# A one-core attention and MLP kernel: each engine's sequence and each tile's buffer taken from two tables instead of from a planner

## The chip, the core and the metric

The kernel runs on one core of a Trainium2 chip. A core has five engines that run their own instruction queues side by side and wait for each other through semaphores: TensorE (PE, matrix multiplies; its weight loads are listed apart as PEld), VectorE (DVE), ScalarE (ACT), GpSimd (POOL) and SyncE (SP, which here only issues DMAs). Each engine takes its instructions strictly in the order in which the program lists them; so an instruction that waits holds up all that stand behind it on that engine. SBUF is the working memory, PSUM the eight banks into which PE writes.

The metric is the device time of one execution in microseconds (us). Before the change the median of 3 runs is 272.35 us (272.06 to 272.52).

## The reference, cut to what matters

```python
batch, n_heads, seq, head_dim = (4, 8, 768, 64)

def _attn_ref(q, k, v):
    chunk = 32; nc = S // chunk; top_k = 6
    k_chunks = k.reshape(B, H, nc, chunk, D)
    k_min = np.min(k_chunks, axis=3)
    k_max = np.max(k_chunks, axis=3)
    ub = np.sum(np.maximum(q * k_min, q * k_max), axis=-1)      # per query and chunk
    ub = np.where(causal, ub, -1000000000.0)
    top_chunks = np.argsort(ub, axis=-1)[..., -top_k:]
    scores = scale * np.matmul(q, k.transpose(0, 1, 3, 2))
    mask = sel & (pos[:, None] >= pos[None, :])                 # sel: key's chunk is chosen
    attn = softmax(np.where(mask, scores, -1000000000.0))
    return np.matmul(attn, v)

def _moe_ref(x, w_in, w_out):       # x: 3072 tokens x 512; d_ff = 2048
    h = x @ w_in
    g = np.where(h > 0.0, h, np.exp(np.minimum(h, 0.0)) - 1.0)
    return g @ w_out
```

Attention over the six best chunks of 32 keys for each query, then an MLP with ELU on the result.

## The kernel before, in words

**Units.** The 32 heads (4 batches of 8) are handled as 16 *pairs* u = 0 to 15; four pairs make a batch. Rows are handled in two *halves* of 384 (hf = 0, 1). Below, K0 is the K load of pair 0 in its first half and K0' in its second; Q and V likewise.

**Stages.** For the first batch (pairs 0 to 3) `first_prep` loads K, Q and V of one half each (L701 and L710), turns each K or Q block on PE with an identity matrix (L730, here called a *turn*), and copies the result out of PSUM with ACT (L759 for K as `lhs`, L779 for Q as `qt`, L784 for its positive part `qa`); DVE takes the minima and maxima of the chunks (L765), POOL copies Q into `rhs` (L799 to L801) and V into `vext` (L792). For the other batches `pair_prep` loads the two K and Q blocks in small pieces (L623), and DVE turns them (L636, L654). `quad_sel` works for two pairs at once: PE makes the bounds (L821 to L833), DVE transposes them, finds the sixth largest (L862) and marks the chunks below it (L867, L873), POOL copies these marks into `rhs` (L884, the *selection copies*). `pair_attend` makes scores on PE (L921 to L931), exponentials on ACT (`pt`, L952), the causal edge on POOL (L971) or PE, the product with V on PE (PV, L979 to L984), the division on DVE (L997, L1000), a transpose on PE (L1009) and its copy by ACT (`xT`, L1012). `mlp` then makes, per batch and half, 16 up-projections (L1034; groups of four matmuls), the ELU on ACT and DVE (L1044 to L1078), 12 down-projection parts for three blocks of rows (L1097), a copy by ACT (`osb`, two buffers, L1105) and the store (L1109 on SP). The weights w_in and w_out come in four parts each by DMAs that POOL issues (L592, L596), each held back until a given product of the first batch exists (`gates`).

**Queues.** Nearly all loads and all stores are issued by SP; ACT issues the two Q loads of pairs 0 and 1. The order on SP is the order of the transfers' issue; a load whose buffer isn't free holds up everything behind it on SP.

**Buffers.** Every tile has a class with a fixed number of buffers (`caps`): 3 `stage`, 9 `pt`, 3 `e`, 2 `osb`, 8 `xT` and so on. PSUM's eight banks are four pairs: pair 0 always holds wide tiles (two banks), pair 1 single ones, pairs 2 and 3 change between both uses; `part` makes a new pool at each such change.

**What sets the order.** The program first records 1706 operations with `add`: engine, an estimated duration, a priority, what they read and write, the buffers that they take and free. Then `Plan.order` (L187) plays a list scheduler: it holds clocks for the engines, a picture of the DMA queues and of instruction fetches, and takes at each step the operation that could start first, ties by priority; a table `RANKS` shifts the priorities of some 300 operations beforehand. It returns the operations in order, each with the buffer numbers that it got, and the program emits them in that order.

Of the kernel before, what the change touches and what calls it, by code (L numbers as in the profile page):

```python
# [42 lines left out]
def WHEN(q_in, left, out):  # L43
# [7 lines left out]
WARM = 8  # L51
# [7 lines left out]
RANKS = ((0, 1, 127), (11, 1, 71), (17, 1, -43), (33, 1, -100), (37, 1, -51), (48, 1, 127), (49, 1, -12),  # L59
# [54 lines left out]
DUMP = None  # L114
# [5 lines left out]


class Plan:

    LAT = {"PE": 0.21, "ACT": 0.17, "DVE": 0.13, "POOL": 0.08, "SP": 2.2, "POOLQ": 2.5}

    BEGIN = 0.85  # L130
    COLD = 7.0
    RING = 2560
    LANES = 8
# [1065 lines left out]
```

## Time and profile before

| what | value |
|---|---|
| median of 3 runs | 272.35 us (272.06 to 272.52) |
| the profiled execution, first to last instruction | 276.5 us, 4.15 us above that median |
| mean granted clock of PE over the span | 0.974 of full speed |
| PE, DVE, ACT, POOL busy | 96%, 72%, 73%, 45% of the span |
| DMA | 29.81 MB, mean 108 GB/s |
| longest waits on PE | 1.3 us (DVE memset ahead of the warming matmuls), then 0.8 us and less |

How to read it: a busy share is that of instructions in flight; matmuls overlap, and a PE that is busy is not at its peak. The granted clock is a row of its own. In timelines, the brackets at a line's end give the idle time of the engine ahead of it and what ended that. SP's lines show when a DMA was issued, not when it landed.

### The profile page before, as it was taken

Reading aid. Unit: us, or ns where it says so; the run is one execution under the profiler, and the core shown is the slowest. Engines: PE = TensorE matmul, PEld = TensorE weight load, DVE = VectorE, ACT = ScalarE, POOL = GpSimd, SP = SyncE. Lnnn points to the kernel's source line nnn. Section 1 sums busy time; section 2 is a strip of 40 time slices with the busy share of each in tenths; the row PEclk is TensorE's granted clock in tenths of the full one; section 3 lists DMA queues with packets and bytes.
Section 4 is the critical chain, followed back from the end, with each engine's and each line's share of the span. In section 5 each row is a group of like instructions: output and inputs, shape, how many; then the busy total and the mean of one; then the engine's idle time right before and its main releaser. Section 6 shows DMA issues by size and latency. Waiting matters only on the chain.

```text
span 276.5 us, 6918 instructions
## 1 busy us (share of the span) xinstructions
PE 266.1 (96%) x2573; PEld 165.0 (60%) x2600; DVE 198.8 (72%) x526; ACT 202.8 (73%) x382; POOL 124.5 (45%) x219
## 2 busy tenths in 40 slices
PE   8889998899999999999999999999999999999995
PEld 4778855565555565655556565666556655555544
DVE  5944686995998998799699953876884846615920
ACT  2956799994797899988979989779579744435411
POOL 5783182794687499766537776010062200000000
PEclk9965899999999999999999999999999999999999
DMA  7999989499997999999974301101010111011022
GB/s 183 235 236 189 189 124 167 73 162 152 149 235 112 199 149 183 177 173 153 158 168 79 78 2 38 40 0 40 10 70 0 40 39 38 28 51 38 2 76 76
DMA packets 111473, 29.81 MB, mean 108 GB/s; under 512 B 101072, under 2 KB 108496, under 8 KB 111440
## 3 DMA queue, kind: packets, MB, share of 16 engines
q1 hardware_dynamic: 106800, 24.78, 48.2%
q0 software_dynamic: 4224, 4.19, 9.8%
q8 instruction: 20, 0.33, 0.5%
q10 hardware_dynamic: 416, 0.39, 0.5%
q14 instruction: 13, 0.11, 0.1%
HBM read 27.26 MB, written 6.29 MB: 121 GB/s over the span
## 4 chain that ended last, share of the span: by engine, by line
PE 71%; DMA 10%; DVE 5%; ACT 5%; issue 3%; SPq 2%; POOL 2%; ACTq 0%; DVEq 0%; POOLq 0%
PE psM L1097 17%; PE psH L1034 15%; PE psS L925 10%; PE psS L1034 8%; PE psMT L1097 7%; PE psO L984 6%; DMA gT<-in_q_dram 4%; DMA w_out_sb<-in_moe_w_out_dram 3%; ACT pt L952 2%; PE psS L833 2%; PE psT L1009 2%; PE psH L735 2%; DMA stage<-in_q_dram 2%; DMA stage<-in_k_dram 1%; SPq L712 1%
## 5 line engine op out<-in xcount | busy, mean ns | idle before, releaser
L952 ACT ACTIVATE pt<-psS 128x768 bf16<-128x768 f32 (+1 forms) x120 | 90.0, 788 | 9.1 <-PE psS L925 7.8
L1034 PE MATMUL psH<-xT,w_in_sb 128*128 128x384 bf16 x384 | 72.9, 325 | 0.1
L1097 PE MATMUL psM<-w_out_sb,gT 128*128 128x512 bf16 x264 | 68.2, 379 | 1.6 <-DMA w_out_sb<-in_moe_w_out_dram 0.2
L1034 PEld LDWEIGHTS <-w_in_sb 128*128 128x128 bf16 x512 | 48.2, 97 | 32.8 <-issue 0.9
L971 POOL TENSOR_SCALAR_AFFINE_SELECT pt<-pt 128x256 bf16<-128x256 bf16 (+1 forms) x56 | 28.8, 518 | 65.5 <-ACT pt L952 64.2
L925 PE MATMUL psS<-rhs,lhs 88*128 88x384 bf16 (+4 forms) x304 | 55.3, 292 | 1.6 <-ACT pt L952 0.7
L1097 PEld LDWEIGHTS <-gT 128*128 128x128 bf16 x400 | 37.1, 97 | 33.0 <-issue 1.2
L1044 ACT ACTIVATE e<-psH 128x384 f32<-128x384 f32 x96 | 47.0, 513 | 8.9 <-PE psH L1034 7.2
L925 PEld LDWEIGHTS <-lhs 88*128 88x128 bf16 x304 | 28.8, 101 | 17.0 <-issue 2.5
L984 PEld LDWEIGHTS <-pt 128*128 128x128 bf16 x672 | 28.5, 99 | 9.6 <-issue 1.7
L1073 DVE SCALAR_TENSOR_TENSOR t<-e,psH 128x384 bf16<-128x384 f32 x48 | 25.5, 545 | 12.1 <-ACT e L1044 11.9
L801 POOL CAST rhs<-qt 64x768 bf16<-64x768 f32 (+1 forms) x40 | 27.9, 701 | 13.3 <-ACT qt L779 11.5
L884 POOL COPY rhs<-selt 24x576 bf16<-24x576 bf16 (+2 forms) x40 | 22.6, 564 | 25.0 <-DVE selt L873 23.3
L984 PE MATMUL psO<-vext,pt 128*128 128x65 bf16 x672 | 32.1, 196 | 0.3 <-POOL pt L971 0.2
L1052 DVE SCALAR_TENSOR_TENSOR gT<-e,psH 128x384 bf16<-128x384 f32 x48 | 25.3, 540 | 9.7 <-ACT psH L1049 9.6
L1044 ACT ACTIVATE e<-psS 128x768 f32<-128x768 f32 x16 | 13.0, 810 | 18.4 <-PE psS L1034 18.4
L1078 DVE SCALAR_TENSOR_TENSOR gT<-psH,t 128x384 bf16<-128x384 f32 x48 | 25.5, 545 | 0.5
L1049 ACT ACTIVATE psH<-psH 128x384 f32<-128x384 f32 x48 | 24.5, 522 | 0.0
L801 POOL CAST lhs<-kt 64x768 bf16<-64x768 f32 x24 | 19.9, 831 | 6.7 <-DVE kt L636 4.5
L1034 PE MATMUL psS<-xT,w_in_sb 128*128 128x384 bf16 x128 | 22.4, 326 | 0.0
L1097 PE MATMUL psMT<-w_out_sb,gT 128*128 128x512 bf16 (+1 forms) x109 | 22.1, 348 | 0.2
L1012 ACT ACTIVATE xT<-psT 128x384 bf16<-128x384 bf16 x32 | 15.8, 501 | 8.6 <-PE psT L1009 8.5
(66 smaller groups left out, 287.6 us busy)
## 6 DMA issues: line engine op xcount, KB each, us to landing
out_dram<-osb SPq DMA_DIRECT2D x23, 256.0 KB, 2.0
stage<-in_k_dram SPq DMA_DIRECT2D x48, 96.0 KB, 3.6
stage<-in_q_dram SPq DMA_DIRECT2D x48, 96.0 KB, 3.8
vd<-in_v_dram SPq DMA_DIRECT2D x12, 384.0 KB, 4.7
w_in_sb<-in_moe_w_in_dram POOLq DMA_DIRECT2D x4, 512.0 KB, 8.4
w_out_sb<-in_moe_w_out_dram POOLq DMA_DIRECT2D x4, 512.0 KB, 9.5
gT<-in_v_dram SPq DMA_DIRECT2D x16, 96.0 KB, 5.1
gT<-in_k_dram SPq DMA_DIRECT2D x6, 192.0 KB, 5.0
```

Of the source, the lines that this page charges most:

```text
L801: nc.gpsimd.tensor_copy(out=o, in_=i)
L925: nc.tensor.matmul(p_s[:, hd, pc:pc + w], lhsT=tiles[pt_["kb"]][0:64 + NCH, hd, 128 * kb:128 * kb + 128], rhs=tiles[pt_["qb"]][0:64 + NCH, ...
L952: lambda bs=bs, pt=pt, wtot=wtot, lo=lo, at=at: nc.scalar.activation(out=tiles[pt][:, :, lo:lo + wtot], in_=tiles[bs[0]][:, :, at:at + wto ...
L971: nc.gpsimd.affine_select(out=a, in_=a, compare_op=AOT.is_ge, fill=0.0, base=0, pattern=pat, channel_multiplier=-1)
L984: nc.tensor.matmul(po[:, hd, qi, :], lhsT=tiles[pt][:, hd, off:off + 128], rhs=tiles[pt_["vx"]][:, 6 * hd + kb, :], start=(kb == 0), stop= ...
L1034: nc.tensor.matmul(ph, lhsT=w_in_sb[:, kk, f0:f0 + 128], rhs=tiles[XT[4 * b + kk]][:, c0:c0 + HALF], start=(kk == 0), stop=(kk == NKK - 1))
L1044: lambda e=e, view=view: nc.scalar.activation(out=tiles[e][:, 0:step], in_=view(), func=AF.Exp),
L1049: lambda view=view: nc.scalar.activation(out=view(), in_=view(), func=AF.Relu),
L1052: lambda e=e, view=view, fc=fc, gt=gt: nc.vector.scalar_tensor_tensor(out=tiles[gt][:, fc:fc + step, :], in0=tiles[e][:, 0:step], scalar=1 ...
L1073: lambda e=e, t=t, view=view: nc.vector.scalar_tensor_tensor(out=tiles[t][:, 0:step], in0=tiles[e][:, 0:step], scalar=1.0, in1=view(), op0 ...
L1078: lambda t=t, view=view, fc=fc, gt=gt: nc.vector.scalar_tensor_tensor(out=tiles[gt][:, fc:fc + step, :], in0=view(), scalar=0.0, in1=tiles ...
L1097: nc.tensor.matmul(pm, lhsT=tiles[gt][:, fc, 128 * tt:128 * tt + 128], rhs=w_out_sb[:, fc, cs], start=(fc == 0), stop=(fc == NFC - 1))
```

## The change

The planner is taken out: `RANKS`, the constants of its clock, DMA and fetch pictures, the hook `DUMP`, and the whole body of `order`. In their place stand two tables: `ORDER` lists the 1706 operations by number in the order in which they are emitted, and `SLOTS` lists the buffer of each tile in the order of its taking. The operations themselves, their shapes, their reads and writes, the buffer counts and every other constant are unchanged.

```diff
-RANKS = ((0, 1, 127), (11, 1, 71), (17, 1, -43), (33, 1, -100), (37, 1, -51), (48, 1, 127), (49, 1, -12),
...
-DUMP = None
+ORDER = (
+    0, 4, 13, 33, 3, 15, 31, 6, 67, 185, 49, 1, 2, 51, 69, 19, 10, 169, 11, 17, 7, 43, 20, 8, 21, 221, 9, 25, 44,
...
+)
+
+SLOTS = (
+    0, 1, 2, 0, 2, 3, 0, 0, 0, 4, 1, 0, 1, 0, 5, 1, 0, 0, 1, 0, 3, 2, 1, 1, 2, 0, 2, 6, 3, 1, 1, 1, 7, 1, 2, 2, 0,
...
+)
...
     def order(self):
-        ops = self.ops
-        for first, n, shift in RANKS:
-            for o in ops[first:first + n]:
-                o.prio += 0.02 * shift
...
-        return out
+
+        left = iter(SLOTS)
+        return [(self.ops[i], [(h, next(left)) for h in self.ops[i].alloc]) for i in ORDER]
...
     steps = plan.order()
-    if DUMP is not None:
-        DUMP(steps)
     with tc.manual_schedule():
```

The lines of the changed kernel stand some 163 lower than those of the kernel before (L706 is L543, L1097 is L934).

Set against the order that the planner gives, each engine has the same operations in another sequence:

| engine | operations | mean shift in places | largest shift |
|---|---|---|---|
| PE | 574 | 3.2 | 22 |
| DVE | 368 | 2.3 | 21 |
| ACT | 383 | 2.5 | 44 |
| POOL | 205 | 4.4 | 40 |
| SP | 83 | 2.4 | 19 |

The head of SP's queue (places 1 to 26; each V of this part is two DMAs):

```
before  K0 K1 Q2 V0 K2 K3 Q3 V1 V2 V3 Q0' K1' Q1' K0' Q3' K3' K2' Q2' V3' V1' V0' V2' K4 Q4 Q5 K5
after   K0 K1 K3 K1' K2 Q2 Q3 Q0' V0 K3' Q2' V2 K0' V1 Q1' V3 K2' Q3' V0' V1' V2' Q5 K4 K5 Q4 V3'
```

The head of PE's queue (places 0 to 21; t: turn, s and S: first and second scores of a pair's first half, ub: bounds of two pairs, pv: the product with V):

```
before  tK0 tQ1 tK1 tQ0 tK2 tQ2 tK3 tQ3 s1 ub01 s2 s0 tQ0' s3 ub23 tK1' S0 S1 tK0' pv0 pv0 tQ1'
after   tK0 tQ1 tQ0 tK1 tK2 tQ2 tK3 tQ3 s1 ub01 tK1' tQ0' s0 s2 ub23 tK0' S0 s3 S1 tQ1' pv0 pv1
```

On POOL the eight requests for weights stand at places 13, 14, 30, 31, 42, 43, 56, 57 before and at 14, 26, 27, 32, 45, 48, 58, 61 after. On SP the first store moves from place 32 to 38, behind the loads K8, K9, Q8 and Q9, of which none stood ahead of it. The first up-projection keeps its place 55 on PE.

More of the change, by code (lines that the diff above doesn't have):

```diff
@@ L128 @@
     LAT = {"PE": 0.21, "ACT": 0.17, "DVE": 0.13, "POOL": 0.08, "SP": 2.2, "POOLQ": 2.5}
[L130 to L133, printed above, removed]
-    FETCH = (120, 256, 4.5, 0.95, 434, 1.5)
-    SHARE = {"SP": 1.0, "ACT": 1.0, "POOL": 0.64}
-    WAKE = 1.2
     def __init__(self, caps):
@@ L187, in order @@
     def order(self):
-        ops = self.ops
-        for first, n, shift in RANKS:
-            for o in ops[first:first + n]:
-                o.prio += 0.02 * shift
-        for o in ops:
-            o.left = len(o.deps) + len(o.after)
-            o.ready = 0.0
-            o.start = o.end = None
-            for d in o.deps:
-                d.users.append(o)
-            for d in o.after:
-                d.followers.append(o)
-        free_slots = {c: [(0.0, i) for i in range(n)] for c, n in self.caps.items()}
@@ L201, in order @@
-        banks = [0.0] * self.caps["ps"]
-        held = {}
-        engines = {}
-        def back(h, t):
-            if h[0] == "ps":
-                banks[held[h]] = t
-            elif h[0] == "S2":
-                banks[2 * held[h]] = banks[2 * held[h] + 1] = t
-            else:
-                free_slots[h[0]].append((t, held[h]))
-        def vacant(c):
-            if c == "ps":
-                return min(banks[2:])
-            if c == "S2":
-                return min(max(banks[i], banks[i + 1]) for i in range(0, len(banks), 2) if i != 2)
-            return min(free_slots[c])[0] if free_slots[c] else 1e18
@@ L220, in occupy @@
-        def occupy(c, r):
-            if c == "ps":
-                i = min((i >= 4 and banks[i ^ 1] < 1e17, banks[i], i) for i in range(2, len(banks))
-                        if banks[i] <= r + 1e-6)[2]
-                banks[i] = 1e18
-                return i
-            if c == "S2":
-                i = min((max(banks[i], banks[i + 1]), i) for i in range(0, len(banks), 2) if i != 2)[1]
-                banks[i] = banks[i + 1] = 1e18
-                return i // 2
-            fs = free_slots[c]
-            s = min(x for x in fs if x[0] <= r + 1e-6)
-            fs.remove(s)
-            return s[1]
@@ L234, in order @@
-        waiting = {}
-        for o in ops:
-            if o.eng == "DMA":
-                continue
-            waiting.setdefault(o.eng, [])
-            engines[o.eng] = self.BEGIN
-            if not o.left:
-                waiting[o.eng].append(o)
-        n_left = sum(o.eng != "DMA" for o in ops)
-        port = {"POOL": 0.0, "DVE": 0.0}
-        out = []
-        parts = {}
-        stalls = []
-        taken, asked = 2 * WARM, self.FETCH[0]
-        queues = {"SP": [], "ACT": [], "POOL": []}
@@ L249, in order @@
-        now = 0.0
-        lands = []
-        def begin(o, k, t):
-            lane = o.lane + k - self.LANES
-            t = max(t, 0.0 if o.issues.dma[0] == "POOL" or lane < 0 else lands[lane])
-            return t + o.dur / o.issues.dma[3]
-        def rate():
-            return 16.0 / sum(q[0][0].dma[1] * self.SHARE[e] for e, q in queues.items() if q)
-        def until():
-            t = 1e9
-            busy = any(queues.values())
-            if busy:
-                t = now + min(q[0][1] / self.SHARE[e] for e, q in queues.items() if q) / rate()
-                for a, b in stalls:
-                    if a <= now < b:
-                        t = b
-                    elif now < a < t:
-                        t = a
-            for e, (o, k, at) in parts.items():
-                d = o.issues
-                q = queues[d.dma[0]]
-                over = sum(x[1] for x in q) + d.dma[2] / d.dma[3] - self.RING
-                if over <= 0 or not q:
-                    t = min(t, max(at, now))
-                elif over <= q[0][1] and not any(a <= now < b for a, b in stalls):
-                    t = min(t, max(at, now + over / (rate() * self.SHARE[d.dma[0]])))
-            return t
@@ L280, in release @@
-        def release(o):
-            for u in o.users:
-                u.left -= 1
-                if u.eng == "DMA":
-                    continue
-                lag = 0.0 if u.eng == o.eng and o.eng in ("PE",) else o.lat
-                u.ready = max(u.ready, o.end + lag)
-                if not u.left:
-                    waiting[u.eng].append(u)
-        def landed(o, t):
-            o.end = t
-            for h in o.free:
-                back(h, t + o.lat)
-            release(o)
-        def move(t):
-            nonlocal now
-            if any(queues.values()):
-                r = 0.0 if any(a <= now < b for a, b in stalls) else rate() * (t - now)
-                for e, q in queues.items():
-                    if q:
-                        q[0][1] -= r * self.SHARE[e]
-                now = t
-                for q in queues.values():
-                    if q and q[0][1] < 1e-6:
-                        o, _, k = q.pop(0)
-                        if o.dma[0] != "POOL":
-                            lands[o.lane + k - 1] = t + o.lat
-                            for e, (i, j, at) in parts.items():
-                                if i.issues.dma[0] != "POOL" and i.lane + j - self.LANES == o.lane + k - 1:
-                                    parts[e] = (i, j, max(at - 1e9, t + o.lat) + i.dur / i.issues.dma[3])
-                        if k == o.dma[3]:
-                            landed(o, t)
-            now = t
-            for e, (o, k, at) in list(parts.items()):
-                d = o.issues
-                q = queues[d.dma[0]]
-                n = d.dma[2] / d.dma[3]
-                if at <= t and (not q or sum(x[1] for x in q) + n <= self.RING + 1e-6):
-                    k += 1
-                    q.append([d, n, k])
-                    if k == d.dma[3]:
-                        del parts[e]
-                        if e in engines:
-                            o.end = engines[e] = t
-                            release(o)
-                    else:
-                        parts[e] = (o, k, begin(o, k, t))
@@ L401, in order @@
-        while until() < 1e8:
-            move(until())
-        return out
+        left = iter(SLOTS)
+        return [(self.ops[i], [(h, next(left)) for h in self.ops[i].alloc]) for i in ORDER]
 @with_exitstack
```

71 lines of the change are left out of this document (removed), and 165 rows, old and new, of tables (ORDER, RANKS, SLOTS).

## The prediction

> **What bounds the kernel now.** I read the page first, then the busy time by stretch, and last the timeline of the first 35 us.
>
> ```profile
> span 276.5 us, 6918 instructions
> PE 266.1 (96%) x2573; PEld 165.0 (60%) x2600; DVE 198.8 (72%) x526; ACT 202.8 (73%) x382; POOL 124.5 (45%) x219
> PEclk9965899999999999999999999999999999999999
> PE 71%; DMA 10%; DVE 5%; ACT 5%; issue 3%; SPq 2%; POOL 2%; ACTq 0%; DVEq 0%; POOLq 0%
> ```
>
> TensorE (PE) is busy nearly throughout and makes 71% of the chain that ended last, so the end comes when PE's fixed work plus PE's losses are through. The operations stay the same; only losses can change. The clock row shows one kind of loss, in slices three to five. The stretches place it:
>
> ```profile
> core 0: us, PE busy (x) PEld busy (x) DVE busy (x) ACT busy (x) POOL busy (x), PEclk, DMA share, GB/s
> 4.80:16.20 11.40, 9.42 (x204) 8.57 (x204) 9.67 (x33) 8.43 (x23) 8.11 (x16) 1.00 1.21 236
> 16.20:29.60 13.40, 13.40 (x168) 11.77 (x167) 5.48 (x21) 8.32 (x18) 6.49 (x14) 0.50 1.02 199
> 29.60:34.70 5.10, 5.10 (x121) 4.21 (x120) 3.77 (x22) 4.04 (x9) 1.00 (x2) 0.98 1.25 202
> 34.70:63.00 28.30, 26.58 (x267) 16.04 (x268) 24.79 (x62) 27.20 (x52) 19.36 (x34) 1.00 0.92 134
> 63.00:155.00 92.00, 90.62 (x898) 53.91 (x908) 82.68 (x217) 78.76 (x155) 62.73 (x99) 1.00 0.97 159
> 155.00:221.00 66.00, 65.41 (x604) 40.33 (x612) 45.53 (x130) 52.85 (x97) 22.66 (x38) 1.00 0.08 27
> ```
>
> For 13.4 us PE runs at half its clock, which costs 6.7 us of full-rate work. Then ScalarE (ACT) is the full one up to 63 us (27.20 of 28.30). From 63 us on PE alone is full: 1.38 us idle of 92, then 0.59 of 66. So whatever the first 35 us lose or win should pass through to the end.
>
> ```profile
> 6.03 0.83 PE L735 MATMUL psMT<-ident_f,gT 96*64 96x96 f32 x16
> 6.69 0.83 PE L735 MATMUL psH<-ident_f,gT 96*64 96x96 f32 x16
> 13.17 0.24 PE L925 MATMUL psS<-rhs,lhs 88*128 88x192 bf16 x1 [0.64 <-DVE ubt L855]
> 13.80 0.24 PE L925 MATMUL psS<-rhs,lhs 88*128 88x192 bf16 x1
> 15.16 0.88 PE L735 MATMUL psMT<-ident_f,gT 96*64 96x96 f32 x16 [0.79 <-DMA gT<-in_q_dram]
> 34.67 1.64 PE L1034 MATMUL psH<-xT,w_in_sb 128*128 128x384 bf16 x9
> 6.00:7.00 1.00, 1.00 (x30) 1.00 (x27) 1.00 (x5) 0.74 (x2) 0.00 (x0) 1.00 1.28 239
> 16.00:17.00 1.00, 1.00 (x26) 0.90 (x32) 0.00 (x0) 0.85 (x3) 0.37 (x2) 0.58 1.25 214
> 29.00:30.00 1.00, 1.00 (x16) 0.90 (x12) 0.00 (x0) 0.25 (x1) 0.00 (x0) 0.60 1.23 210
> ```
>
> A turn (one K or Q block transposed) takes 0.66 us from start to start, a group of first scores 0.63 (13.17 to 13.80). PE stands 0.64 us before 13.17 and 0.79 us before 15.16; about 1 us after the second hole the clock falls, and it comes back at 29.6. The first MLP matmul starts at 34.67. The second hole is a wait for the load of Q of pair 0, second half.
>
> **The change part by part.** The planner's run costs no device time. Each engine issues the same operations with the same shapes, so the sum of durations does not move.
>
> *Head of the SP queue.* Before, K and Q of the second halves stand behind all four first V loads:
>
> ```profile
> 2.23 0.98 SPq L712 DMA_DIRECT2D gT<-in_v_dram  x2
> 4.92 0.50 SPq L706 DMA_DIRECT2D gT<-in_q_dram  x1
> 6.09 3.61 SPq L712 DMA_DIRECT2D gT<-in_v_dram  x6
> 9.74 0.49 SPq L706 DMA_DIRECT2D gT<-in_q_dram  x1
> 10.28 0.45 SPq L706 DMA_DIRECT2D gT<-in_k_dram  x1
> 11.28 1.43 SPq L706 DMA_DIRECT2D gT<-in_k_dram  x1
> gT<-in_q_dram SPq DMA_DIRECT2D x4, 192.0 KB, 5.3
> ```
>
> The awaited Q of pair 0 is issued at 9.74, as SP's 15th DMA; landing takes 5.3 us. After, it is the 8th, the place that is issued at 4.92 now: landed near 10.2 instead of 15.0. K of pair 1, second half, moves from 10.28 to the fourth place, issued near 2.2 and landed near 7.5. K2, Q2, K3 and Q3 swap places among the same seven, so the first ten entries of PE keep their pace. V moves back; its reader on PE, the first PV, moves from place 19 to 20 only, and V of pair 1 drops from the 8th to the 14th load, a place issued at 11.28 now, so landed near 16.6. Its PV stands at place 21, which PE reaches near 18.7 (below): covered by 2 us.
>
> *Head of PE.* After the tenth entry, at 12.53 (13.17 less 0.64), come now two turns whose data has landed, 1.3 us of work, in place of the holes. Both holes close: 0.64 + 0.79 = 1.43 us. Bounds: 0 (their banks or ACT are not ready) and 1.43.
>
> *ACT behind it.* The turns' results leave through ACT:
>
> ```profile
> L759 ACT ACTIVATE lhs<-psH 64x384 bf16<-64x384 f32 x15 | 7.2, 483 | 6.3 <-PE psH L735 6.2
> L779 ACT ACTIVATE qt<-psMT 128x384 f32<-128x384 f32 x7 | 3.4, 490 | 3.0 <-PE psMT L735 3.0
> ```
>
> ACT is busy 8.43 + 8.32 + 4.04 = 20.8 us of the 29.9 up to 34.7, so 9.1 us idle, mostly waiting for turns; 1.5 us of that lies before its first copy, at 6.26 by the row of 6 to 7 us, which must wait for the first load. ACT could be through 7.6 us sooner, at 27.1. PE's work left at 16.2 is 13.4 x 0.5 + 5.1 = 11.8 us at full rate; less 1.43 it is 10.4, so PE could be through at 26.6. The two are neck and neck. The first PV waits for the 30th activation: 20.8 us over 50 instructions is 0.42 each, so about 6.3 + 12.5 = 18.8 us. PE reaches it at 12.53 + 4 turns (2.6) + six score or bound groups of 0.6 (3.6) = 18.7. From there PE waits for ACT step by step, and I take it that the clock falls then, at 19.6, and comes back at 29.6 as before. Then 3.4 us run at full rate (7.0 left), 10.0 at half (2.0 left), and the first MLP matmul starts at 31.6: **3.1 us earlier**. If the low stretch keeps its 13.4 us, or falls at 16.2 again, 0.3 or 3.7 us are left at its end, and both end at 33.3: 1.4 us earlier.
>
> [...] In the trace the clock fell after holes of 0.64 and 0.79 us and stayed down through 13.4 us in which PE shows no idle time. [...]
>
> *The weights' requests on POOL.*
>
> ```profile
> L592 POOL DMA_DIRECT2D w_in_sb<-in_moe_w_in_dram x4: 746/746/921, 12.4 to 26.6; - x4
> DMA to landing us min/median/max: 5.7/8.4/11.7
> 88.86 0.65 PE psH L1034 x4
> ```
>
> The second part of w_in is asked for twelve places later, behind eight selection copies, two V copies and a cast. Its new place lies between the first and last requests, 12.4 and 26.6; taken at 22, it lands at 30.4 (27.7 to 33.7). It is needed four groups of 0.65 us after the first, at 34.2. Cost taken: 0; other bound: asked at 26.6 with the longest landing it comes at 38.3, 4.1 us late, and the up-projections queued behind it on PE wait with it.
>
> *Stores behind loads.* The first output store moves from SP place 32 to 38, behind four loads.
>
> ```profile
> 75.64 0.48 SPq L1109 DMA_DIRECT2D out_dram<-osb  x1
> 86.48 3.55 SPq L623 DMA_DIRECT2D stage<-in_k_dram  x4
> 101.06 0.60 ACT L1105 ACTIVATE osb<-psM 128x512 f32<-128x512 f32 x1
> ```
>
> Its buffer is wanted again by the fourth copy to that tile, at 101.06. The store would go after the load whose issues end at 90.03 and one more (3 us), so near 93, 8 us ahead of that copy: cost 0; without that cover ACT, and PE behind it, would stand.
>
> *Buffers, the middle, the tail.* PSUM bank pairs change between wide and single use 30 times before and after; the nearest wait for such a bank:
>
> ```profile
> PE psS L925 <- ACT pt L952: 0.7, 2, 0.5
> 265.92 7.34 PE psMT L1097 x49
> ```
>
> Two waits, 0.7 us in all: taken as 0, bounds -0.7 and +1. From 34.7 to 221 PE idles 1.72 + 1.38 + 0.59 = 3.7 us; entries shift by 3 places in the mean. I take 0, with bounds -1.5 (under half of it closes) and +1.5. The tail is the same closing run of down-projections (7.34 us); the last two output halves are interleaved, and the first half's copy still ends ahead of the last one's: 0.
>
> Sum: -3.1. On the profiled execution 276.5 - 3.1 = 273.4; it stands 4.15 above the median of the runs, 272.35, from which I take the same: **269.3**.
>
> **The rivals.**
> (B) *The clock holds.* PE never falls to half rate: it is through at 26.6, ACT at 27.1; with a fifth of ACT's 7.6 us idle left, 28.6, so -6.1: 266.3. For it: both holes before the fall go. Against it: PE at full rate outruns ACT from 19 us on.
> (C) *Hidden anyway.* The chain of waits, in order of time, passes through w_out:
>
> ```profile
> 54.20 8.94 DMA w_out_sb<-in_moe_w_out_dram
> 63.19 1.02 PE psM L1097 x4
> ```
>
> The start is won, but the stretch ends at 63.2 where it did, because a part of w_out sets it; after the change two of its requests stand three and five places later on POOL. Against it: PE takes up the parts of w_out later too (third part: place 119 to 125). Gain 0: 272.3.
> (D) *A second fall, slower.* At the head of the MLP, 34 to 50 us, ACT is full, so PE stands whenever a score group or w_in comes late. Where holes reach some 1.4 us within 3 us (what preceded the fall at 16.2), the clock falls once more for 13.4 us: +6.7, less the 1.72 us that PE idles there anyway: +5.0, against -3.1: 274.3. For it: the later w_in request and four score groups now put ahead of up-projections. Against it: up-projections are long and dense, and nothing fell there before.
>
> **How the numbers follow.** Chances: forecast 0.38 (its own range 267.9 to 271.0: gains of 1.4 to 4.4), B 0.21, C 0.12, D 0.26, other 0.03. No change is within 0.2%, 0.54 us. Faster: forecast, B and a third of C, 0.63; same: most of C, 0.08; slower: D and the rest, 0.29. The range 266.0 to 275.2 leaves out under half of B and the upper third of D.
>
> **What would show it.** Right: no hole over 0.3 us between 12.5 and 16 us on PE's timeline; Q of pair 0 landing near 10; clock still 1.00 at 17 us; the first line of up-projections near 31.6; stretches after 63 us with PE as full as now. Forecast against B: one low stretch, beginning near 19.6. D: a second row of low clock after 34 us. Wrong altogether: first up-projection at 34 or later, or PE idle past 63 us grown by over 1.5 us.

## The result, and the profile after

The ratio of the changed kernel to the one before, measured side by side, is 0.9941 with a 95% interval of 0.9918 to 0.9965: faster by 0.6%, or 1.6 us on 272.35, which puts it near 270.7 us. Forecast were 3.1 us and 269.3. Ratios here compare the executions within 1.5% of the fastest of their own kernel; that leaves out nine of 20 before and eight of 20 after, three of these at full clock (272.79 to 273.81 us), with which the gain would be 0.5%.

The page of the changed kernel: span, busy time, granted clock in 40 slices, and the chain that ended last by engine.

```profile
span 270.9 us, 6867 instructions
PE 260.2 (96%) x2572; PEld 160.1 (59%) x2600; DVE 202.6 (75%) x526; ACT 202.9 (75%) x382; POOL 123.4 (46%) x219
PEclk9999999999999999999999999999999999999999
PE 78%; DMA 6%; ACT 6%; DVE 5%; issue 3%; SPq 1%; POOL 0%; ACTq 0%; DVEq 0%
```

The low slices of the clock row are gone. The same stretches as before the change (columns: length, then PE, PEld, DVE, ACT and POOL busy, clock, DMA share, GB/s):

```profile
core 0: us, PE busy (x) PEld busy (x) DVE busy (x) ACT busy (x) POOL busy (x), PEclk, DMA share, GB/s
4.80:16.20 11.40, 10.62 (x253) 9.56 (x254) 10.16 (x36) 9.38 (x24) 6.59 (x14) 1.00 1.19 247
16.20:29.60 13.40, 11.59 (x234) 9.73 (x233) 9.55 (x44) 10.39 (x25) 7.34 (x16) 1.00 1.20 207
34.70:63.00 28.30, 27.62 (x319) 17.34 (x321) 25.87 (x77) 24.92 (x48) 16.43 (x29) 1.00 0.99 148
63.00:155.00 92.00, 89.85 (x858) 53.60 (x869) 84.20 (x216) 82.21 (x157) 60.50 (x94) 1.00 0.92 149
155.00:221.00 66.00, 65.57 (x596) 40.05 (x603) 46.10 (x109) 49.23 (x90) 24.20 (x41) 1.00 0.11 35
```

The timeline of PE in the head, where the prediction closes its two holes, and the line of the up-projections ("issue" marks idle time in which the engine waited for nothing that the profile shows):

```profile
12.38 0.88 PE L572 MATMUL psH<-ident_f,gT 96*64 96x96 f32 x16
13.10 0.83 PE L572 MATMUL psMT<-ident_f,gT 96*64 96x96 f32 x16
15.23 0.20 PE L762 MATMUL psS<-rhs,lhs 88*128 88x64 bf16 x1 [0.50 <-issue]
```

```profile
L871 PE MATMUL psH<-xT,w_in_sb x66: 323/326/337, 29.8 to 59.9; 128*128 128x384 bf16 x66
```

Read against the old profile much is won: two turns stand at 12.38 and 13.10 where PE stood idle, the clock is full, and the first up-projection starts 4.9 us earlier. Yet the time fell by 1.6 us only. The numbers fit together with one fact: the profiled execution of before has its clock at half for 13.6 us, and the three runs behind 272.35 us don't have that stretch. The changed kernel's execution of 272.62 us has a span of 270.9, so a time stands 1.7 us above its span, and a span of 276.5 belonged to a time of about 278.2. The next thing to get was therefore a second profile of the old order.

### The profile page after: what moved, and what is told of

Its sections match the earlier page's. It is cut to its first block, busy times and chain, and to the rows that moved or that the text cites. A ratio compares the mean times of both kernels' runs of the same rounds, so it can differ in the third digit from the quotient of the medians.

```text
span 270.9 us, 6867 instructions
## 1 busy us (share of the span) xinstructions
PE 260.2 (96%) x2572; PEld 160.1 (59%) x2600; DVE 202.6 (75%) x526; ACT 202.9 (75%) x382; POOL 123.4 (46%) x219
## 4 chain that ended last, share of the span: by engine, by line
PE 78%; DMA 6%; ACT 6%; DVE 5%; issue 3%; SPq 1%; POOL 0%; ACTq 0%; DVEq 0%
PE psM L934 19%; PE psH L871 18%; PE psS L762 10%; PE psS L871 8%; PE psMT L934 8%; PE psO L821 6%; DMA w_out_sb<-in_moe_w_out_dram 3%; PE psS L670 3%; PE psH L572 2%; ACT pt L789 2%; PE psT L846 2%; DMA stage<-in_q_dram 2%; DMA out_dram<-osb 2%; PE nothing L997 1%; PE psMT L572 1%
## 5 line engine op out<-in xcount | busy, mean ns | idle before, releaser
L789 ACT ACTIVATE pt<-psS 128x768 bf16<-128x768 f32 (+3 forms) x120 | 88.8, 776 | 8.5 <-PE psS L762 6.2
L934 PE MATMUL psM<-w_out_sb,gT 128*128 128x512 bf16 x264 | 68.8, 379 | 2.2 <-ACT osb L942 1.0
L871 PEld LDWEIGHTS <-w_in_sb 128*128 128x128 bf16 x512 | 47.6, 97 | 33.5 <-issue 1.2
L934 PEld LDWEIGHTS <-gT 128*128 128x128 bf16 x400 | 37.3, 97 | 34.9 <-issue 1.9
L881 ACT ACTIVATE e<-psH 128x384 f32<-128x384 f32 x96 | 46.4, 501 | 12.8 <-PE psH L871 9.8
L762 PE MATMUL psS<-rhs,lhs 88*128 88x384 bf16 (+4 forms) x304 | 53.5, 283 | 1.2 <-issue 0.9
L821 PEld LDWEIGHTS <-pt 128*128 128x128 bf16 x672 | 30.7, 98 | 10.4 <-POOL rhs L638 0.5
L762 PEld LDWEIGHTS <-lhs 88*128 88x128 bf16 x304 | 26.6, 97 | 14.9 <-issue 2.4
L821 PE MATMUL psO<-vext,pt 128*128 128x65 bf16 x672 | 34.8, 194 | 0.1
L638 POOL CAST rhs<-qt 64x768 bf16<-64x768 f32 (+1 forms) x40 | 27.7, 696 | 13.7 <-ACT qt L616 9.9
L889 DVE SCALAR_TENSOR_TENSOR gT<-e,psH 128x384 bf16<-128x384 f32 x48 | 25.5, 544 | 4.5 <-ACT psH L886 4.2
L881 ACT ACTIVATE e<-psS 128x768 f32<-128x768 f32 x16 | 12.9, 810 | 16.4 <-PE psS L871 16.2
L886 ACT ACTIVATE psH<-psH 128x384 f32<-128x384 f32 x48 | 23.6, 501 | 0.0
L934 PE MATMUL psMT<-w_out_sb,gT 128*128 128x512 bf16 (+1 forms) x108 | 21.6, 347 | 0.2
L899 DVE TENSOR_SCALAR t<-e 128x768 bf16<-128x768 f32 x16 | 8.9, 558 | 16.0 <-ACT e L881 15.7
```

What stands on the lines that cost most here:

```text
L638: nc.gpsimd.tensor_copy(out=o, in_=i)
L762: nc.tensor.matmul(p_s[:, hd, pc:pc + w], lhsT=tiles[pt_["kb"]][0:64 + NCH, hd, 128 * kb:128 * kb + 128], rhs=tiles[pt_["qb"]][0:64 + NCH, ...
L789: lambda bs=bs, pt=pt, wtot=wtot, lo=lo, at=at: nc.scalar.activation(out=tiles[pt][:, :, lo:lo + wtot], in_=tiles[bs[0]][:, :, at:at + wto ...
L821: nc.tensor.matmul(po[:, hd, qi, :], lhsT=tiles[pt][:, hd, off:off + 128], rhs=tiles[pt_["vx"]][:, 6 * hd + kb, :], start=(kb == 0), stop= ...
L871: nc.tensor.matmul(ph, lhsT=w_in_sb[:, kk, f0:f0 + 128], rhs=tiles[XT[4 * b + kk]][:, c0:c0 + HALF], start=(kk == 0), stop=(kk == NKK - 1))
L881: lambda e=e, view=view: nc.scalar.activation(out=tiles[e][:, 0:step], in_=view(), func=AF.Exp),
```

## The experiments

All kernels below have the operations of the two kernels; only the sequence of the engines (and, where it must, a buffer number) differs. They are written as tables. A table needs only 1613 of the 1706 recorded operations: the other 93 are landings of DMAs, which no engine executes, and the changed kernel's `ORDER` doesn't list them. Ratios are to the kernel before, run beside them.

| run | head (206 operations) | behind it | ratio | 95% interval |
|---|---|---|---|---|
| e1 | old | old | 0.9973 | 0.9939 to 1.0008 |
| e2 | new | old | 1.0031 | 0.9987 to 1.0075 |
| e3 | old | new | 0.9953 | 0.9904 to 1.0002 |
| e4 | new | new (the changed kernel) | 0.9946 | 0.9901 to 0.9991 |
| e5 | new | new, stores ahead | 0.9956 | 0.9920 to 0.9993 |
| e6 | old | new, stores ahead | 0.9988 | 0.9949 to 1.0027 |
| e7 | old | new for 185 operations, then old | 1.0067 | 1.0035 to 1.0099 |
| e8 | old | old for 185 operations, then new | 0.9993 | 0.9972 to 1.0015 |
| e9 | new | new, V3' ahead | 0.9897 | 0.9860 to 0.9933 |
| e10 | new | new, V3' and stores ahead | 0.9930 | 0.9901 to 0.9960 |
| e11 | old | new, V3' and stores ahead | 0.9960 | 0.9933 to 0.9987 |
| e12 | old | old, one selection ahead | 1.0049 | 1.0032 to 1.0066 |
| e13 | old, loads of SP new | old | 1.0333 | 1.0306 to 1.0360 |
| e14 | old | new, V3' ahead | 0.9927 | 0.9902 to 0.9952 |
| e15 | new | new, V3' ahead (e9 again) | 0.9921 | 0.9899 to 0.9943 |

### Where the gain is: e1 to e4

```diff
 # HEAD: what both orders issue ahead of operation 363, the first up-projection
-ORDER = NEW
+e1: ORDER = OLD
+e2: ORDER = [n for n in NEW if n in HEAD] + [n for n in OLD if n not in HEAD]
+e3: ORDER = [n for n in OLD if n in HEAD] + [n for n in NEW if n not in HEAD]
```

> The order and buffers of before, written as tables: every engine issues the same instructions in the same sequence as before, so a ratio of 1.000 within 0.003. It is a second profile of the old order. Theory 1 (the half-rate stretch from 16.2 to 29.6 belongs to the one execution profiled before and not to the 272.35 runs, whose time stands about 1.7 above its span): granted clock 1.00 from 16 to 30, first up-projection between 28.5 and 31.0 rather than at 34.67, span about 270.5. Theory 2 (the stretch belongs to the old order, as the prediction had it): about 13 us at 0.50 ahead of 30 again, first up-projection at 34 to 35, span about 276.

> The new order for the 206 operations issued ahead of the first up-projection, the old order behind them, the old buffers everywhere. If the gain of 1.6 us comes from the head (the order of the loads and the turns, as predicted): ratio 0.994. If it comes from what is behind the head: 1.000. If the head gains more and the rest gives back: 0.988, a first up-projection at 29.8 and PE as full between 70 and 84 as in the old order.

> The old order for the 206 operations of the head, the new order and the old head's buffers, then the new order behind it. If the gain comes from the head: 1.000, first up-projection where the old order has it. If it comes from behind the head: 0.994. If the two parts don't add (the new middle needs the new head's times): above 1.000.

> The changed kernel once more, on the chip of the three others, as the measure for them: ratio 0.994 within 0.003. Theory 1: its granted clock is 1.00 throughout in this second profile too, first up-projection at 29.8 within 0.3. Theory 2 adds nothing here.

The old order's second profile, e1: page and stretches.

```profile
span 270.0 us, 6945 instructions
PEclk9999999999999999999999999999999999999999
```

```profile
4.80:16.20 11.40, 9.17 (x236) 8.24 (x232) 9.84 (x33) 9.10 (x24) 8.29 (x17) 1.00 1.21 250
16.20:29.60 13.40, 12.97 (x268) 10.75 (x251) 10.13 (x45) 12.10 (x28) 7.41 (x17) 1.00 1.21 221
63.00:155.00 92.00, 91.61 (x877) 53.93 (x875) 85.48 (x223) 81.79 (x158) 64.13 (x101) 1.00 0.91 151
```

```profile
L876 PE MATMUL psH<-xT,w_in_sb x64: 323/326/337, 28.8 to 50.1; 128*128 128x384 bf16 x64
```

Theory 1 holds: full clock from 16.2 to 29.6, a span of 270.0, and a first up-projection at 28.8, which is 1.0 us *earlier* than in the changed kernel. At full clock the head had nothing of 3.1 us to give. e2, the new head alone, is no faster than before; e3, with the old head, has most of the changed kernel's gain. So the gain arises behind the head, though the interval of e3 alone still reaches 1.0002.

To see where, PE's progress can be added up: each matmul that has started counts with the usual spacing of its shape (162 ns for an up-projection, 216 ns for a down-projection, and so on: in the changed kernel's profile a group of four of the first kind at 111.50 us takes 0.65 us to the next group's start, one of the second kind at 114.32 takes 0.86). The lead over e1, in us of PE work, from four profiles that, like e1's, hold all 2600 matmuls; what spacing the small matmuls are given changes these figures by about 0.1:

| at, us | 24 | 30 | 48 | 72 | 84 | 96 | span of e1 less this span |
|---|---|---|---|---|---|---|---|
| e2 new head, old rest | 0.4 | -1.1 | -1.4 | -1.9 | -1.8 | -1.6 | -1.7 |
| e3 old head, new rest | -0.2 | -0.2 | 1.1 | 0.9 | 1.0 | 1.4 | 1.2 |
| e4 new order | 0.8 | -0.5 | 1.2 | 1.1 | -0.8 | -0.3 | -0.5 |
| e15 new order, V3' ahead | 0.3 | -1.1 | 0.5 | 0.5 | 0.8 | 1.2 | 1.1 |

The lead at 96 is the difference of the spans within 0.2 us: from there on PE is full whatever the order. Four things stand in the table. From 24 to 30 the new head loses 1.3 to 1.5 us, wherever its rest comes from (the hole behind this is in the last section). From 30 to 48 the three kernels with the new rest gain 1.3 to 1.7 us. From 84 to 96 they gain another 0.4 to 0.5. And e4 gives 1.9 us back between 72 and 84, e3 and e15 nothing: the new order has accidents, in some executions.

### The gain from 30 to 48: e7, e8, e12

In e1, PE's losses there follow a stretch in which VectorE stands (third column of busy times). The stretch in e1:

```profile
36.00:38.00 2.00, 1.90 (x27) 1.10 (x33) 0.55 (x1) 2.00 (x6) 0.68 (x3) 1.00 1.05 146
40.00:42.00 2.00, 1.32 (x8) 0.41 (x7) 1.94 (x15) 1.68 (x3) 0.00 (x0) 1.00 1.41 212
46.00:48.00 2.00, 1.50 (x10) 0.82 (x10) 2.00 (x4) 2.00 (x5) 1.87 (x4) 1.00 0.75 121
```

And in e4:

```profile
36.00:38.00 2.00, 2.00 (x16) 1.26 (x14) 1.91 (x17) 2.00 (x6) 0.15 (x1) 1.00 0.93 146
40.00:42.00 2.00, 2.00 (x34) 1.50 (x33) 2.00 (x6) 2.00 (x6) 1.93 (x5) 1.00 0.13 22
46.00:48.00 2.00, 2.00 (x36) 1.50 (x33) 1.97 (x4) 1.87 (x4) 0.38 (x1) 1.00 1.20 195
```

VectorE works 0.55 us of 2 in the old order at 36 and 1.91 in the new; PE then loses 0.68 us of 2 at 40 and 0.50 at 46 in the old, nothing in these rows of the new (0.35 us from 42 to 44, against 0.04 in the old). What VectorE does at 36 in the new order is the block selection of pairs 2 and 3, second half, which the table puts eight places earlier on PE and five to seven on VectorE. e7 and e8 cut the orders at the first down-projection; e12 moves that selection alone.

```diff
 # MID: the 391 operations that both orders issue ahead of operation 427
+e7:  ORDER = [HEAD from OLD] + [MID less HEAD from NEW] + [the rest from OLD]
+e8:  ORDER = [MID from OLD] + [the rest from NEW]
 # e12, on OLD:
-PE:  ... 255, 383, 387, 249, 251, 391, 403, 258, 261, 262, 395, 293, ...
+PE:  ... 255, 293, 383, 387, 249, 251, 391, 403, 258, 261, 262, 395, ...
-DVE: ... 382, 386, 393, 389, 394, 294, 390, 267, 295, 268, 296, 405, 297, 406, 298, ...
+DVE: ... 382, 294, 295, 296, 386, 393, 297, 389, 394, 298, 390, 267, 268, 405, 406, ...
```

> Old head, the new order for the 185 operations between the head and the first down-projection (about 30 to 52 us), the old order and so the old places of the stores behind them. Theory 4 (the gain is made between 36 and 48, where VectorE stands idle from 35.5 to 37.2 in the old order and TensorE pays for it from 40 to 47): lead over the old order 0.7 to 1.1 us at 66, kept to the end, ratio 0.996 to 0.997. Rival (the gain is made behind 52): 1.000.

> The old order for the 391 operations ahead of the first down-projection, the new order behind them. Theory 4: no lead at 66; the late store then costs 0 to 1.9 us at 76 to 84 and 0.5 us comes back between 92 and 102: ratio 0.999 to 1.004. Rival (the gain is made behind 52): 0.994 to 0.996.

> The old order with one thing of the new: the block selection of the last first job stands nine places earlier on TensorE and up to five places earlier on VectorE; three buffers of PSUM pairs change with it. Theory 4 (VectorE stands idle from 35.5 to 37.2 in the old order, this work then comes late and TensorE pays from 40 to 47): VectorE idle under 1 us between 35 and 38, lead over the old order 0.5 to 1.0 us at 66, ratio 0.996 to 0.998. Rival (the gain needs the whole new order behind the head): 0.999 to 1.003.

By the ratios theory 4 fails in e7 (slower by 0.7%) and in e12 (slower by 0.5%); e8 came out as it said, and as "no gain" would have. e8's profile holds a half-rate stretch, so no lead can be read from it. e7's profile has the lead of 1.1 us at 48 and then loses it; its longest waits from 48 to 66 are ones that neither whole order has (a wait of PE: line, what ended it, us in all, times, longest):

```profile
PE psM L935 <- DMA w_out_sb<-in_moe_w_out_dram: 1.3, 2, 1.1
```

The new middle asks for w_out later (first at 40.09 us in e7, at 33.30 in e1), the old rest wants it as early as ever. In e12 the selection done early pushes other work back; PE waits 2.2 us in three places from 30 to 48:

```profile
PE psS L675 <- ACT pt L794: 0.8, 1, 0.8
PE psS L767 <- DVE gT L920: 0.8, 1, 0.8
PE psO L826 <- POOL pt L813: 0.6, 1, 0.6
```

So it is shown where the gain arises and that VectorE is then busy, not that any one move makes it. That the order there wins only as a whole is the reading left; no run shows what in it does.

### The late store: e5, e6

In the changed kernel PE waits at 83. SP's timeline, then ACT's, then PE's:

```profile
78.31 0.47 SPq L946 DMA_DIRECT2D out_dram<-osb  x1
```

```profile
82.63 0.60 ACT L942 ACTIVATE osb<-psM 128x512 f32<-128x512 f32 x1 [1.62 <-DMA out_dram<-osb]
```

```profile
83.28 1.02 PE L934 MATMUL psM<-w_out_sb,gT 128*128 128x512 bf16 x3 [0.96 <-ACT osb L942]
```

The first two copies to `osb` were made at 65.3 and 65.8; the first store was issued at 78.31, behind the eight loads of K8 and K9, and landed at 82.6. Only then has the third copy a buffer, and PE its bank. e4 has the same, with 1.5 us.

```diff
-SP: ... 564, 943, 960, 439, 581, 945, 962, 432, 598, 977, 991, 446, ...
+SP: ... 564, 439, 432, 943, 960, 581, 945, 962, 446, 598, 977, 991, ...
```

> The changed kernel with three of SP's requests moved ahead and nothing else: the first two stores of the result stand ahead of the two groups of four K loads that they stood behind, the third two places ahead. Theory 3 (in the new order a finished copy waits some 12 us on SP for its store, the next copy waits for its buffer, and TensorE waits 1.0 to 1.5 us for that copy at about 82): no wait of the down-projection for the copy between 74 and 86, the lead of about 1 us that the new order has at 72 is kept, span 268.6 to 269.3, ratio 0.989 to 0.991. Rival (the four K loads behind the stores are as tight): they land 1.2 us later, TensorE waits for their turns instead, ratio 0.994 to 0.997.

> As the third run (old order in the head, new order behind it), with the same three stores moved ahead. If the head is worth nothing, as the third run against the changed kernel says: the ratio of the run beside it within 0.002. If the new head is worth what the prediction gave it with the clock left out (some 1.4 us of closed holes): 0.005 above that ratio.

(439, 432 and 446 are the stores; the third passes three loads.) Theory 3 predicted 0.989 to 0.991 for e5; it measured 0.9956, no better than e4, and e6 is not better than e3, whose profile has no wait at 83 to begin with. Nor has e6's, but it has another, at 56. POOL's timeline of e6, SP's, and PE's:

```profile
51.28 0.76 POOL L434 DMA_DIRECT2D w_out_sb<-in_moe_w_out_dram  x1
56.36 0.50 POOL L630 CAST vext<-gT 128x384 bf16<-128x384 f32 x1 [1.96 <-DMA gT<-in_v_dram]
```

```profile
50.87 1.06 SPq L550 DMA_DIRECT2D gT<-in_v_dram  x2
```

```profile
56.91 0.19 PE L822 MATMUL psO<-vext,pt 128*128 128x65 bf16 x1 [1.22 <-POOL vext L630]
```

In e5's profile the wait at 83 is gone, and the same V load cost more. PE's timeline of e5, and its stretches:

```profile
57.51 0.22 PE L822 MATMUL psO<-vext,pt 128*128 128x65 bf16 x1 [4.39 <-POOL vext L630]
```

```profile
55.00:56.00 1.00, 0.00 (x0) 0.00 (x0) 0.00 (x0) 0.00 (x0) 0.00 (x0) 0.66 1.52 214
62.00:63.00 1.00, 1.00 (x34) 0.39 (x19) 0.33 (x1) 0.00 (x0) 0.00 (x0) 0.92 0.72 117
```

PE stands for 4.39 us, and the clock is at half from 55.3 to 62.2.

### The V load beside the weights: e9, e10, e11

V3', the last V load of the first batch, stands at place 18 of SP before the change and at 25 behind it (the table of heads in the section on the change has it last). In the old order it is issued ahead of 25 us; in the new one behind Q4, at about 50, beside POOL's request for the third quarter of w_out. Its second transfer and that request start within a few tenths of a us, and which comes first varies: in e3 V was first by 0.09 us and landed in 2.6 us; in e6 the weights were first by 0.16 us and it landed in 4.8, POOL waited 1.96 us, and PE 1.22; in e5 they were first by 0.40 us and it landed in 7.7. So the 96 KB of V (sizes from the DMA issues on the changed kernel's page) took about twice as long where the request for 512 KB of weights had begun 0.16 us ahead, and three times as long where it had begun 0.40 us ahead; how the DMA engines divide their time between the two, no run shows.

```diff
-SP: ... 171, 189, 207, 552, 533, 550, 535, 225, 567, ...
+SP: ... 171, 189, 207, 552, 225, 533, 550, 535, 567, ...
```

(225 is V3'; 552, 533, 550, 535 are Q5, K4, K5, Q4.) e10 adds the edit of e5; e11 is e10 with the old head, where V3' stands behind 207.

> The changed kernel with one SP request pair moved: the last V load of the first jobs (two transfers, behind four Q loads in the new order, issued at about 50 beside the third quarter of w_out) goes three places ahead, behind the first four Q loads of the next jobs. Theory 5 (in the new order these two transfers and the w_out request start within 0.1 to 0.4 us of each other at 49 to 51; where the weights come first the V load lands 5 to 8 us after its issue instead of 2.6, and TensorE waits up to 4.4 us for the block built from it): no wait for that block between 48 and 60 in the profile, the runs of the kernel lie within 2.5 us of each other, ratio 0.989 to 0.992. Rival (its transfers only take the place of the K loads behind them, which are as tight): 0.994 to 0.997.

> The same V load ahead and the three stores of the fifth run ahead as well. If the late store costs TensorE what the profiles of the changed kernel show at 82 (1.0 to 1.5 us): 0.003 to 0.005 below the ratio of the run beside it, 0.986 to 0.988. If the loads behind the stores give it back: the same ratio within 0.002.

> The old order in the head, the new order behind it, with the V load and the stores ahead as in the run beside it. With the two accidents gone the two heads are compared cleanly. The prediction's step (1.43 us of closed holes ahead of 16 reach the first up-projection): 0.004 to 0.005 above the run beside it. Theory 4 (the holes are closed but ScalarE and VectorE set the pace to 30, so the head is worth nothing): within 0.002 of it.

e9 gives 0.9897, inside theory 5's figures and the lowest ratio measured, with a span of 267.0 in its profile; run again as e15 it gives 0.9921, just outside them. With the two longest of its nine executions (272.62 and 272.99 us), which the ratio leaves out, e9's mean is 0.992 of the kernel beside it, as in e15. Both ratios lie below the changed kernel's 0.9941 and 0.9946, though the intervals overlap. The spread expected, 2.5 us, is missed in e9 (268.2 to 273.0) and held in e15 (269.6 to 270.8). POOL's timeline of e9 shows the same block made without a wait:

```profile
49.01 0.76 POOL L434 DMA_DIRECT2D w_out_sb<-in_moe_w_out_dram  x1
52.06 0.51 POOL L630 CAST vext<-gT 128x384 bf16<-128x384 f32 x1
```

Moving the stores as well gains nothing (e10). In e9 and e15 the store keeps its place, but SP reaches it sooner (74.99 and 76.42 instead of 78.31) and PE no longer waits there. e10 against e11 sets the heads apart by 0.003, as e5 against e6 does: less than the 0.004 to 0.005 of the closed holes, more than the 0.002 of no difference, and in both pairs the intervals overlap.

### The head at full clock: e13, e14, e15

```diff
 # e13, on OLD, the first places of SP
-SP: 13, 31, 51, 17, 49, 67, 69, 35, 53, 71, 169, 185, 187, 167, 223, 221, 203, 205, 225, 189, 171, 207
+SP: 13, 31, 67, 185, 49, 51, 69, 169, 17, 221, 205, 53, 167, 35, 187, 71, 203, 223, 225, 171, 189, 207
 # e14: as e11, with the stores left in their places
```

(17, 35, 53 and 71 are V0 to V3; 185 is K1', 169 Q0'.)

> The old order with the one edit of the head that the prediction built its sum on: SP's first loads stand in the new sequence (the loads of the second jobs' K and the next jobs' Q ahead of the V loads), everything else as before. The prediction's sum (holes of 0.64 and 0.79 us closed, the clock held): ratio 0.987 to 0.990. Theory 4 with the clock left out (the holes close or move, ScalarE and VectorE set the pace to 30): 0.998 to 1.001, first up-projection at 28.5 to 29.2 as in the second profile of the old order; the load of the next Q lands at 10 to 11 instead of 14.4.

> The old order in the head, the new order behind it, the V load ahead (at the old order's own place in the head's tail), the stores as in the new order. Theory 4: the head is worth nothing beyond what the instruction stream does to it, ratio within 0.002 of the run beside it (e15). If the new head is worth the 1.43 us of holes: 0.004 to 0.006 above it.

> The changed kernel with the last V load of the first jobs ahead, once more, as the measure for the run beside it. Theory 5: ratio 0.989 to 0.992, no run with the wait at 53 to 57. Theory 6 (runs of this order fall into two groups 1.5 to 2 us apart: in one, the third block of instructions is fetched at about 26 instead of 22.5 and TensorE stands 1.0 to 1.2 us at 27 with nothing to execute): the profile shows the hole at 27 and an up-projection at 29.3 where the fetch is late, no hole and 27.9 where it is early.

e14 and e15 differ in the head alone and measure 0.9927 and 0.9921. e14's figure rests on two of its six executions (270.32 and 270.37 us); the other four, the profiled one among them, stand at 275.38 to 276.61 us with a mean clock of 0.975. Over all five pairs the new head differs from the old by 0.001 to 0.003 for the better in front of the new rest and by 0.006 for the worse in front of the old (e1, e2), and every pair of intervals overlaps: at full clock it is worth nothing that can be told. In e15's profile the lead of the new head is lost again by 30 (-1.1).

The ratios leave one thing out. A mean clock of 0.973 to 0.975, which is what one stretch of 13.6 us at half leaves of a span of some 276 us, stands in 56 of 198 executions with the old head (the kernel before, run beside e1 to e15, and e1, e3, e6 to e8, e11, e12, e14; in none of e12's nine) and in 1 of 82 with the new one (the changed kernel, e2, e4, e5, e9, e10, e15). The stretch goes with the old head, as the prediction had it; which of the head's edits removes it, no run shows.

e13 was the surprise: not 0.987 to 0.990, not 1.000, but 1.0333. Q0' lands at 10.5 as wanted. The waits of its PE ahead of 20 us, POOL's timeline, and its stretches:

```profile
PE psS L767 <- POOL rhs L643: 3.2, 3, 1.2
PE psS L767 <- DVE ubt L697: 0.6, 1, 0.6
```

```profile
11.34 0.51 POOL L634 CAST vext<-gT 128x384 bf16<-128x384 f32 x1 [5.93 <-DMA gT<-in_v_dram]
11.79 3.09 POOL L643 CAST rhs<-qt 64x384 bf16<-64x384 f32 x6
16.52 0.51 POOL L634 CAST vext<-gT 128x384 bf16<-128x384 f32 x1 [1.64 <-DMA gT<-in_v_dram]
```

```profile
15.00:16.00 1.00, 0.64 (x9) 0.67 (x10) 0.91 (x10) 0.98 (x4) 0.00 (x0) 0.77 1.26 242
...
24.00:28.00 4.00, 4.00 (x43) 3.45 (x43) 1.19 (x3) 2.55 (x5) 1.09 (x4) 0.50 0.85 152
...
31.00:32.00 1.00, 1.00 (x13) 0.97 (x11) 0.67 (x2) 1.00 (x4) 0.63 (x2) 0.50 0.68 39
32.00:33.00 1.00, 1.00 (x18) 0.86 (x17) 0.17 (x2) 0.98 (x3) 0.00 (x0) 0.69 1.20 200
```

In the old order POOL copies V0 ahead of all its copies of Q. With the V loads moved back it stands 5.93 us at that copy, six copies of Q queue behind it, and PE's scores wait for them, 3.2 us in three waits. Two of these (1.14 and 1.16 us) and the wait for `ubt` (0.64) stand ahead of 15.5; there the clock falls, and it stays at half to 32.6: 17.1 us, worth 8.5 of the 9.1 us that 1.0333 means. A fall of the clock behind holes, on which the prediction built, is real; here it is in all six runs of the kernel (mean clock 0.962 to 0.969). The new order also moves POOL's copies of V behind those of Q, and so needs the loads in that sequence: neither edit can be priced without the other.

## Why the prediction came out as it did

**The failed step: "3.1 us earlier", and with it "it stands 4.15 above the median of the runs, 272.35, from which I take the same".** The 3.1 us are a first up-projection at 31.6 instead of 34.67, and 34.67 holds the half-rate stretch. At full clock the old order has it at 28.8 (e1), the new at 29.8 and 29.3 (the first and second profile). At full clock the head has no gain that can be told (e14 against e15; e2 1.0031). The 4.15 us were no offset: with 1.7 us between span and time, the profiled execution stood about 5.9 us above the median, and the stretch, priced at 6.7 us in the prediction, is all of that and more. A gain that consists of removing something may be taken off only those runs that have it. That the direction came out right is luck as far as the sum goes: the measured gain arises between 30 and 48 us, which the sum put at 0.

*Head of SP.* Right in its numbers: Q0' landed at 10.53 (forecast near 10.2), K1' at 7.61 (7.5).

*Head of PE.* The mechanism was right in part: both turns stand in the holes' place, and nothing over 0.3 us is idle from 12.5 to 14.7. Then comes a new hole, of 0.50 us up to 15.23, without a named cause; e4 has it too, up to 15.14. The price of 1.43 us did not pass on: of it a lead of 0.8 us stood at 24 (e4 over e1), and by 30 a second hole, of 1.23 us at 27 and again marked "issue", had turned it into -0.5. In e5 and e9, which lack this second hole, the first up-projection starts at 27.6 and 27.9, 1.2 and 0.9 us ahead of e1.

*ACT behind it.* That PE would outrun ACT and wait for it step by step was wrong: PE idles 1.81 of 13.40 us from 16.2 to 29.6 in the new profile, but 1.6 of that stand in holes marked "issue" and 0.2 in a wait for ACT. That the clock falls then, at 19.6, was wrong too; it held. So by its own marks the picture was that of rival B (first up-projection 28.6), whose price of 6.1 us was taken from the same wrong base; the measured 270.7 us stand 4.4 above its 266.3.

*The weights' requests on POOL.* Taken at 0, and so it is: the second part was asked for at 20.78, landed at 26.63, and no up-projection waits for it.

*Stores behind loads.* Taken at 0, with the cover named for one store, the copy at 101.06. The mis-sized term is its neighbour: the store that had been second, now first, stands behind K8 and K9, and the *third* copy waits for it, for 1.0 and 1.5 us of PE's time in two profiles. Moving it gained nothing: in e5 V3' came late instead, and e10 had no such wait left to lose, since V3' ahead had taken it away (e9, e15).

*Buffers, the middle, the tail.* Taken at 0 within 1.5 us. This is where the gain is: 1.3 to 1.7 us from 30 to 48 and 0.4 from 84 to 96, less what the accidents cost. The prediction counted shifts by places and looked at no chain in this stretch; ACT full at 27.20 of 28.30 us, on its own page, was also a reading of that one execution (24.27 in e1).

*What was left out.* V3' moving from place 18 to 25 on SP stood in the list of the head and got no term. It costs 0 to 1.2 us of PE's time in the profiles of e3, e4, e6 and the changed kernel, and 4.39 us in e5's; taken back, it brings 0.9946 (e4) to 0.9897 and 0.9921, with overlapping intervals.

*C and D.* C (hidden by w_out at 63.2) was wrong: leads of 1 us pass 63 unchanged. D (a second fall behind 34) didn't come in the two profiles of the changed kernel, but e5's has it: 6.8 us at half behind a wait of 4.39 us for V3'. Three of the changed kernel's 20 executions have mean clocks of 0.981 to 0.988, the size that stretches of this kind leave (0.988 in e5); where they lie, no trace shows.

## What to carry to other kernels

Compare a profile's span with the runs before pricing anything in it: a profiled execution that stands some per cent above the median holds something that the median doesn't (here 13.6 us at half clock), and a gain made of that is no gain in the median. A sequence of one engine is priced together with the in-order sequences of the engines that feed it; e13 has nearly the SP head of the winning order, and it costs 3.3%: POOL's old sequence doesn't fit it. Where two queues issue a small urgent load and a large one within tenths of a us, move the small one well ahead, since which comes first varied here (the small one by 0.09 us in e3, the large one by 0.16 in e6 and 0.40 in e5); that took away waits of up to 4.39 us, and its gain in the ratio, some 0.3%, is within the intervals.

## What the runs showed of the hardware

The half-rate stretches of five profiles have lengths in steps. In the old profile the clock was 0.58 over 16 to 17 and 0.60 over 29 to 30, so it fell at 16.16 and came back at 29.80: 13.6 us. In e13 it was 0.77 over 15 to 16 and 0.69 over 32 to 33: 15.54 to 32.62, 17.1 us. In e8 (16.00 to 29.66) and e14 (15.00 to 28.66) it was 13.7 us each, in e5 6.8. Within 0.1 us these are 4, 5, 4, 4 and 2 times 3.41 us, a quarter of the first; what sets this step, no run shows. A PE busy throughout did not bring the clock back in e13 for over 8 us: the rows for 24 to 28 and 28 to 32 have it busy for 4.00 of 4.00 us each at 0.50, and the clock comes back at 32.62. What does bring it back, no run shows.

The size of the holes alone did not decide whether the clock fell. PE's three longest waits in the old head were 0.8, 0.6 and 0.5 us in the old profile, 0.7, 0.6 and 0.6 in e8 and 0.8, 0.6 and 0.5 in e14, where it fell; they were 1.0, 0.7 and 0.5 in e1 and 0.8, 0.6 and 0.4 in e6, where it held.

In some profiles PE stands with nothing in the profile that it waits for. Profiles of the new head have at about 27 such a hole of 1.0 to 1.2 us, in the middle of a group of transposes, or not. PE's timeline in e4 and the row of the instruction queue from 25.5 to 27.5 us (packets, MB, share):

```profile
28.13 0.38 PE L846 MATMUL psT<-ident_b,on 128*128 128x128 bf16 x4 [1.23 <-issue]
```

```profile
q8 instruction: 1, 0.02, 3.0%
```

PE's timeline in e9, which has no such packet there but one between 22 and 24:

```profile
26.60 0.51 PE L847 MATMUL psT<-ident_b,on 128*128 128x128 bf16 x6
```

Of the six profiles with the new head and the new rest four have the hole of 1.0 to 1.2 us, and all four have the late packet and none between 22 and 24 (the changed kernel, e4, e10, e15); e9, with the early one, has no hole. e5 has no hole either, and e2, with the old rest, has one of 1.2 us. The first up-projection starts at 27.6 and 27.9 without the hole and at 29.3 to 29.9 with it, and the span of e9 is 1.9 us shorter than that of e15, the same kernel; the six times of e15 lie within 1.3 us and don't show two groups. That the late packet causes the hole, PE then lacking instructions, is the author's reading of this agreement; no run changed the packet alone.
